# Scores of an attention head on its own 32 rows of the TensorE array, with three row maxima in the same tiling

## The chip, the cores and the metric

The kernel runs on one core of one Trainium2 chip. The metric is the time of one execution on the device in microseconds (us): 1010.03 us, the median of three runs (1009.28 to 1010.32). One execution was also recorded by the hardware profiler; everything said below of single instructions comes from that record.

## The reference

`x` is 2048 tokens by 448 features. Two attentions are computed from it, each with 16 heads of 28 features, and a gate per token mixes them:

```python
g = sigmoid((x * gate_w).sum(-1, keepdims=True))
a = A(x)     # linear attention: feature maps by two softmaxes per head, then (phi_k^T V), and a quotient
b = B(x)     # softmax attention, all 2048 queries against all 2048 keys, per head:
             #   scores = q @ k^T * 28 ** -0.5;  p = softmax(scores);  o = p @ v;  then @ wo
return g * a + (1 - g) * b
```

Only B is touched by the change. Everything is float32; a product in TensorE's fast format (fp32r) loses low bits, so each factor is split into a high and a low part, and a product of two such factors is high x high + low x high + high x low.

## The kernel before, in words

**Front** (up to about 356 us in the trace): projections of q, k and v, the whole of A, and the first part of the row maxima of B. **Attention loop** (the rest): B, head group by head group. A head group is four heads; a block (`gq`, 16 of them) is one head group with 512 queries; a step (`s`, 256 of them) is one block with 128 keys. Before the loop ends, the last head group's blocks are projected by `wo` (`project`, L1020) and mixed with A.

*Scores* (`scores`, L869). For each of the four heads j, one matmul over all 128 array rows makes scores transposed, 128 keys by 512 queries, in a PSUM bank `st`. The 128 rows are a stack (L840 to L864): 4 groups of 32 rows, which hold, beside the row of the maxima, the parts of k against the parts of q: high, low, high, low of k (`kst`) against high, high, low, low of q (`qst`). So one matmul of 128 rows yields all products of one head at once. Row 0 of `qst` holds the row maximum of each query and row 0 of `kst` holds -1, so that the maximum is subtracted in the same matmul. ScalarE then takes exp of each bank into an SBUF tile `p` (L890).

*Values* (`values`, L1008). For step s-1, four matmuls, each on its own 32 columns of the array (tile_position (0, 32j)), add p times v into one PSUM bank `pv` per block. The operands are plain float32, and the trace shows two passes per matmul, so eight records for one step.

*Row maxima*. The maximum over the 2048 keys must be known before a block's first score. It is taken from scores in one product (high x high, 28 rows). There are two kinds of work for it:
- A *unit* (`mx_unit`, L259) in the front: four matmuls on four groups of 32 array rows make two differences and two scores; ScalarE takes relu of the differences (L291) and VectorE adds and takes the maximum (L292). `NF` = 76 units are done before the loop.
- A *visit* (`mx_visit`, L307) in the loop: four matmuls (L324), one for each head, on four groups of 32 rows, for 128 queries by 512 keys. One bank in four goes by ScalarE (relu, L328) and is joined to another by VectorE (L333); the others are reduced by VectorE straight from PSUM (L336, L342). This uses keys that were differenced by GpSimd before (`take_diffs`). There are 180 visits.

When a block's maxima are complete, VectorE reduces and transposes them (`mx_reduce`, L238), and SyncE's DMA queue copies them into row 0 of `qst` in four DMAs (`load_nm`, L857).

*Order*. The order on TensorE, VectorE, ScalarE and GpSimd is the order of the program; SyncE's queue holds the DMAs. The main loop (L1146) goes by visits: steps 1 to 104 in pairs with one visit a pair, steps 105 to 232 alternately with 5 and 3 heads' scores ahead of a visit (`ahead`, L1145), the last ones in pairs with no visit. One round of it is: scores, values, visit. So TensorE goes through three tilings in a round: 128x128 (scores), 128 rows by 32 columns (values), 32 rows by 128 columns (visit). Of the 8 PSUM banks one is `pv`; the other seven go round among scores and visits (`cycle_banks`, L937).

At the end of a block (`finish`, L1052) VectorE copies `pv` out (L419), the denominators go through DRAM by three DMAs (L422, L433, L434) with a reciprocal on VectorE three steps later (L429), and GpSimd multiplies (L440).

Of the kernel before, what the change touches and what calls it, by code (L numbers as in the profile page):

```python
# [8 lines left out]
F32 = mybir.dt.float32  # L9
# [8 lines left out]
P = 128  # L18
# [11 lines left out]
NF = 76  # L30
LOWEST = -3.0e38
LAST = 232
OUTS = (200, 238, 246, 210)
PROJ = (235, 243, 251)
# [7 lines left out]
def gated_mix_kernel(ctx, tc, xT, wqkB, wvB, wvA, wkAT, wqAT, phi, woA, woB,  # L42
# [141 lines left out]
    diffs = []  # L184

    def mx_load(g, c):
        mxs[("kc", g, c)] = r = mx_tile("kc", f"kc{g}_{c}", 5)
        if c == 0:
            mxs["kd"] = mx_tile("kd", f"kd{g}", 1)
            for h in range(3):  # L190
                mx_rows(mxs["kd"], (h,), k_d[g], (h,), h * 512)
        for h in range(4):
            mx_rows(r, (h,), k_d[g], (h,), 512 * (c + (c == h and c < 3) - (c == h + 1 and c > 0)))
        if c < 3:
            js, t = slice(32 * c, 32 * c + DH), mxs["kd"]
            diffs.append((mxs["u"] + mxs["f"] // 4, lambda: nc.gpsimd.tensor_sub(
                r[js], f32(r[js]), f32(t[js]))))

    def take_diffs(n):
        while diffs and diffs[0][0] + n <= mxs["u"] + mxs["f"] // 4:  # L200
            diffs.pop(0)[1]()
# [33 lines left out]

    GM, QM = NF // 16, NF % 16 // 4

    def mx_reduce(gq):  # L238

        col = 64 * gq  # L240
        if gq < GM:
            parts = [(0, 4, col, 2)]
        elif gq == GM:
            parts = [(0, QM, col, 2), (QM, 4, col + 8 * QM, 4)]
        else:
            parts = [(0, 4, col, 4)]

        def reduce():
            for a, z, c, n in parts:
                nc.vector.tensor_reduce(  # L250
                    red[:, :16].rearrange("p (h t) -> p h t", t=4)[:, :, a:z],
                    part[:, c:c + 4 * (z - a) * n].rearrange("p (k t h) -> p h t k", t=z - a, h=4),
                    AX.X, ALU.max)
            nm_of[gq] = nm = mxp.tile([P, 32], F32, tag="nm", name=f"nm{gq}", bufs=7)
            nc.vector.transpose(nm, f32(red))

        mxs["fin"].append(reduce)

    def mx_unit():  # L259
# [5 lines left out]
        take_diffs(2)  # L265
# [3 lines left out]
        if gq < GM:  # L269
            c, qt = divmod(r, 4)  # L270
            hp, b = divmod(c, 2)
            col = 64 * gq + 16 * b + 4 * qt + 2 * hp
            if r in (4, 9):
                pair_query(gq + 1, r // 9)
        else:
            c, qt = divmod(r, QM)
            hp, b = divmod(c, 2)
            col = 64 * gq + 4 * QM * b + 4 * qt + 2 * hp
            if r == 0:
                mx_query(gq)  # L280
# [13 lines left out]
        if gq < GM and qt == 3 and qb == NQ - 1:  # L294
            pair_load(g + 1, c)
        if gq == GM and qt == QM - 1:
            mx_load(g, c)
        if r == 15:
# [3 lines left out]
    flats = [(GM, kb, qt, h, 64 * GM + 8 * QM + 4 * (4 - QM) * kb + 4 * (qt - QM) + h)  # L302
             for qt in range(QM, 4) for kb in range(4) for h in range(4)]
    flats += [(gq, kb, qt, h, 64 * gq + 16 * kb + 4 * qt + h) for gq in range(GM + 1, NG * NQ)
              for qt in range(4) for kb in range(4) for h in range(4)]

    def mx_visit(mid):  # L307


        take_diffs(2)  # L310
        f = mxs["f"]
        todo = flats[f:f + 4]
        fins = mxs["fin"][:1 if todo and todo[0][1] == 0 else None]
        del mxs["fin"][:len(fins)]
        mxs["f"] = f + len(todo)
        if todo:
            gq, kb, qt, _, col = todo[0]
            g, qb = divmod(gq, NQ)
            if kb == 1 and qt in (0, QM) and gq + 1 < NG * NQ and ("qc", gq + 1) not in mxs:
                mx_query(gq + 1)  # L320
            pm = mx_banks(f, kb)
            for j in sorted(range(4), key=lambda j: j != kb):
                js = slice(32 * j, 32 * j + DH)
                nc.tensor.matmul(pm[j], mxs[("qc", gq)][js, qt * P:(qt + 1) * P],  # L324
                                 mxs[("kc", g, kb)][js, :], start=True, stop=True,
                                 tile_position=(32 * j, 0))
            rl = late_p.tile([P, 512], F32, tag="rl", name=f"rl{f}", bufs=3)
            nc.scalar.activation(rl, pm[kb], AF.Relu if kb < 3 else AF.Copy)  # L328
            seen = 0
            for j in sorted({0, 1, 2, 3} - {kb}, key=lambda j: j == kb - 1):  # L330
                if j == kb - 1:
                    r = mxs["rl"]
                    nc.vector.tensor_tensor_reduce(r, pm[j], r, 1.0, LOWEST, ALU.add, ALU.max,  # L333
                                                   part[:, col + j:col + j + 1])
                else:
                    nc.vector.tensor_reduce(part[:, col + j:col + j + 1], pm[j], AX.X, ALU.max)  # L336
                seen += 1
                if seen == 2:
                    mid()
            mxs["rl"] = rl  # L340
            if kb == 3:
                mxs["fin"].append(lambda: nc.vector.tensor_reduce(  # L342
                    part[:, col + 3:col + 4], rl, AX.X, ALU.max))
            if qb == NQ - 1 and g + 1 < NG:
                if qt == 2 and kb == 3:
                    mx_load(g + 1, 0)
                if qt == 3 and kb < 3:
                    mx_load(g + 1, kb + 1)
            if qt == 3 and kb == 3:
                mx_reduce(gq)  # L350
        for fn in fins:
            fn()
# [487 lines left out]
    def stack(nm, keys):  # L840
        r = at.tile([P, 4, 512], F32R, name=nm)
        nc.gpsimd.memset(f32(r), 0.0)
        if keys:
            nc.gpsimd.memset(f32(r[0:1]), -1.0)
        return r

    def load_stack(r, src, c, parts):
        for b, i in enumerate(parts):
            nc.sync.dma_start(f32(r[32 * b + 4:32 * b + 32]),
                              src[:, i, c:c + 512].rearrange("(j d) n -> d j n", d=DH))  # L850
        return r

    def load_q(gq):
        g, qb = divmod(gq, NQ)
        qst_of[gq] = load_stack(qst[gq % 2], q_d[g], qb * 512, (0, 0, 1, 1))

    def load_nm(gq):  # L857
        nm = nm_of.pop(gq)
        row = f32(qst_of[gq][0:1].rearrange("p a (t b r) -> p (a t) b r", b=4, r=32))
        for b in range(4):  # L860
            nc.sync.dma_start(row[:, :, b, :], nm[32 * b:32 * b + 16, :])

    def load_k(g, kb):
        kst_of[(g, kb)] = load_stack(kst[(4 * g + kb) % 5], k_d[g], kb * 512, (0, 1, 0, 1))  # L864

    NS = NG * NQ * NT
    pv_of, pts, late, mids = {}, {}, {}, {}

    def scores(s, i, js=range(4)):  # L869

        gq, kt = divmod(s, NT)
        g, qb = divmod(gq, NQ)

        def score(j, st):
            nc.tensor.matmul(st, kst_of[(g, kt // 4)][:, j, (kt % 4) * P:(kt % 4 + 1) * P],  # L875
                             qst_of[gq][:, j, :], start=True, stop=True)

        if s == 0:
            for j in (2 * i, 2 * i + 1):
                p, st = at.tile([P, 512], F32, name=f"p{s}_{j}"), ps_mx(f"st{s}_{j}")  # L880
                score(j, st)
                nc.scalar.activation(p, st, AF.Exp, scale=SCALE)
                pts.setdefault(s, []).append(p)
            return
        sts = {j: bank(b, f"st{s}_{j}") for j, b in zip(js, i)}
        for j in js:
            score(j, sts[j])
        for j in js:
            p = late_p.tile([P, 512], F32, tag="p", name=f"p{s}_{j}", bufs=12)
            nc.scalar.activation(p, sts[j], AF.Exp, scale=SCALE)  # L890
            pts.setdefault(s, []).append(p)
# [10 lines left out]
    for t in range(8, NT):  # L902
# [5 lines left out]
        else:  # L908
            value_b(t, lambda i: scores(0, i // 3 - 1) if i in (4, 7) else None)
# [13 lines left out]
    late3, visit = [0, 1, 2], [3, 4, 5, 6]  # L923
    free = []
    spare = []
# [3 lines left out]


    for i in (0, None, 5, 4, 3, 2, 1, 6):
# [5 lines left out]
    def cycle_banks(n):  # L937

        x, y = late3[:], visit[:]
        if spare:  # L940
            b = [(free.append(free.pop(0)), free[-1])[1] for _ in range(n)]
        elif n == 4:
            b = x + y[:1]
            late3[:], visit[:] = [b[2], b[3], y[3]], [b[0], y[1], b[1], y[2]]
        elif n == 3:
            b = x
# [323 lines left out]
```

## Time and profile before

| what | before |
|---|---|
| time, median of 3 runs | 1010.03 us |
| span of the profiled execution, first to last instruction | 1008.5 us |
| time of TensorE matmuls in flight, share of the span | 1002.0 us, 99% |
| ScalarE | 821.3 us, 81% |
| VectorE | 647.5 us, 64% |
| GpSimd | 249.8 us, 25% |
| granted TensorE clock | 1.000 |

The profiled execution has no time of its own beside its span; 1010.03 is 1.5 us more than the span. PE stands for TensorE's matmuls and PEld for its weight loads, which can run beside them; DVE is VectorE, ACT ScalarE, POOL GpSimd, SP SyncE. A matmul's recorded duration reaches from its start to the modelled arrival of its last result, so matmuls overlap and a busy PE says little; start to start is what a matmul costs. Rows of the timeline merge instructions of one kind that follow each other: start, duration from the first start to the last end, engine, line, count, and in brackets the idle time before and what ended it.

### The profile page before, as it was taken

What the parts mean: (1) busy time and instruction counts of PE and PEld (TensorE: products, weight loads), DVE (VectorE), ACT (ScalarE), POOL (GpSimd) and SP (SyncE); (2) the same over time, 40 slices, a digit from 0 to 9 for tenths busy, and PEclk for the clock granted to TensorE, in tenths of its full rate; (3) what the DMA queues carried; (4) which work ended last, traced back from release to release, by engine and by line L of the source; (5) the groups of instructions that cost most, each with busy time, mean ns of one, the idle gap of its engine ahead of it and who ended that gap; (6) DMA issues with size and microseconds to landing.
All of it is one profiled execution on the core that took longest, in us unless ns stands there. A gap on an engine that the chain in (4) does not pass through costs nothing.

```text
span 1008.5 us, 18049 instructions
## 1 busy us (share of the span) xinstructions
PE 1002.0 (99%) x6344; PEld 565.2 (56%) x6344; DVE 647.5 (64%) x1336; ACT 821.3 (81%) x1614; POOL 249.8 (25%) x218
## 2 busy tenths in 40 slices
PE   9999999999999999999999999999999999999998
PEld 7777777877777754444444443333333333335665
DVE  5566777898764635445445468888888788885112
ACT  4455556587866699999999999999999999997662
POOL 1134545679635910310110110010120101100010
PEclk9999999999999999999999999999999999999999
DMA  9873010122233771223542334433232255610441
GB/s 303 300 249 108 32 52 32 43 56 81 80 103 95 174 146 37 67 63 80 113 101 49 72 76 94 107 71 71 68 79 63 68 124 141 148 38 30 137 147 56
DMA packets 64605, 99.64 MB, mean 99 GB/s; under 512 B 18166, under 2 KB 24934, under 8 KB 64514
## 3 DMA queue, kind: packets, MB, share of 16 engines
q1 hardware_dynamic: 64514, 98.49, 37.1%
q8 instruction: 50, 0.82, 0.3%
q14 instruction: 41, 0.34, 0.1%
HBM read 70.29 MB, written 27.78 MB: 97 GB/s over the span
## 4 chain that ended last, share of the span: by engine, by line
PE 92%; DVE 3%; DMA 3%; issue 1%; ACT 1%; SPq 0%; DVEq 0%; ACTq 0%
PE st L875 28%; PE pv L1015 24%; PE pm L324 8%; PE poa L109 4%; PE pk L127 4%; PE pva L127 4%; PE pqk L109 3%; PE pmd L287 3%; PE pob L109 3%; PE pq L109 2%; PE pvb L127 2%; PE pvb L109 2%; DMA qkd<-ev 2%; PE pn L553 1%; DMA xraw<-in_xT_dram 1%; PE pft L541 1%
## 5 line engine op out<-in xcount | busy, mean ns | idle before, releaser
L890 ACT ACTIVATE p<-st 128x512 f32<-128x512 f32 x1020 | 525.1, 639 | 26.4 <-PE st L875 26.4
L336 DVE TENSOR_REDUCE part<-pm 128x1 f32<-128x512 f32 x405 | 258.7, 685 | 179.3 <-PE pm L324 179.2
L875 PE MATMUL st<-qst,kst 128*128 128x512 f32 x1024 | 299.7, 423 | 0.0
L1015 PE MATMUL pv<-p,vb 128*32 128x512 f32 x2048 | 259.7, 601 | 0.0
L875 PEld LDWEIGHTS st<-qst,kst 128*128 128x128 f32 x1024 | 171.1, 187 | 101.3 <-ACT p L890 38.9
L440 POOL TENSOR_TENSOR oUb<-oUb,rsb 128x512 f32<-128x512 f32 x15 | 19.3, 1287 | 494.8 <-DMA rsb<-rdb 262.8
L292 DVE CUSTOM_DVE_ANT_0 rl<-pmb,rl 128x512 f32<-128x512 f32 x152 | 98.0, 682 | 46.6 <-ACT rl L291 46.5
L328 ACT ACTIVATE rl<-pm 128x512 f32<-128x512 f32 x180 | 111.5, 620 | 10.6 <-PE pm L324 10.2
L324 PEld LDWEIGHTS pm<-kc,qc 28*128 28x128 f32 x720 | 34.4, 181 | 150.9 <-ACT p L890 102.3
L291 ACT ACTIVATE rl<-pmd 128x512 f32<-128x512 f32 x152 | 82.9, 601 | 31.7 <-PE pmb L287 29.3
L1015 PEld LDWEIGHTS pv<-p,vb 128*32 128x32 f32 x2048 | 50.4, 108 | 96.2 <-issue 93.9
L333 DVE CUSTOM_DVE_ANT_0 rl<-pm,rl 128x512 f32<-128x512 f32 x135 | 91.8, 680 | 0.0
L324 PE MATMUL pm<-kc,qc 28*128 28x512 f32 x720 | 91.0, 495 | 0.0
L109 PE MATMUL pqk<-XH,wB 128*128 128x512 f32 x192 | 59.4, 397 | 0.8 <-DVE ev L593 0.8
L592 ACT CAST ev<-pqk 128x512 fp32r<-128x512 f32 x28 | 16.0, 588 | 38.9 <-PE pqk L109 21.9
L109 PE MATMUL poa<-woA_s,oTa 128*128 128x448 f32 x192 | 43.4, 375 | 0.0
L1026 DVE SCALAR_TENSOR_TENSOR acc<-pob,gate,acc 128x448 f32<-128x448 f32 x12 | 8.2, 684 | 50.8 <-PE pob L109 50.8
L109 PEld LDWEIGHTS pqk<-XH,wB 128*128 128x128 f32 x192 | 35.3, 188 | 9.8 <-issue 1.5
L287 PE MATMUL pmb<-kp,qp 28*128 28x512 f32 x152 | 39.8, 494 | 0.4
L127 PE MATMUL pk<-wkA_s,XH 128*128 128x448 f32 x128 | 39.4, 381 | 0.0
L109 PEld LDWEIGHTS poa<-woA_s,oTa 128*128 128x128 f32 x192 | 34.9, 188 | 6.2 <-issue 2.9
L593 DVE TENSOR_TENSOR ev<-pqk,ev 128x512 fp32r<-128x512 f32 x28 | 18.9, 689 | 29.9 <-ACT ev L592 29.8
(159 smaller groups left out, 1214.5 us busy)
## 6 DMA issues: line engine op xcount, KB each, us to landing
qkd<-ev SPq DMA_DIRECT2D x28, 512.0 KB
qst<-qkd SPq DMA_DIRECT2D x64, 224.0 KB
kst<-qkd SPq DMA_DIRECT2D x64, 224.0 KB
od<-oTb SPq DMA_DIRECT2D x48, 112.0 KB
rsa<-rda SPq DMA_DIRECT2D x8, 512.0 KB
rsb<-rdb SPq DMA_DIRECT2D x15, 256.0 KB
gad<-ga SPq DMA_DIRECT2D x16, 224.0 KB
acc<-gad SPq DMA_DIRECT2D x4, 896.0 KB
```

The costliest lines, as they stand in the source:

```text
L109: nc.tensor.matmul(dst, l, r, start=i == 0, stop=i == len(todo) - 1)
L127: nc.tensor.matmul(dst[:, :n], l, r, start=i == 0, stop=i == len(todo) - 1, skip_group_check=True)
L287: nc.tensor.matmul(pm[j], qc[js, qt * P:(qt + 1) * P], kc[js, :], start=True, stop=True, tile_position=(32 * i, 0))
L291: nc.scalar.activation(rl, pm[i], AF.Relu)
L292: nc.vector.tensor_tensor_reduce(rl, pm[2 + i], rl, 1.0, LOWEST, ALU.add, ALU.max, part[:, col + i:col + i + 1])
L324: nc.tensor.matmul(pm[j], mxs[("qc", gq)][js, qt * P:(qt + 1) * P], mxs[("kc", g, kb)][js, :], start=True, stop=True, tile_position=(32 * ...
L328: nc.scalar.activation(rl, pm[kb], AF.Relu if kb < 3 else AF.Copy)
L333: nc.vector.tensor_tensor_reduce(r, pm[j], r, 1.0, LOWEST, ALU.add, ALU.max, part[:, col + j:col + j + 1])
L336: nc.vector.tensor_reduce(part[:, col + j:col + j + 1], pm[j], AX.X, ALU.max)
L875: nc.tensor.matmul(st, kst_of[(g, kt // 4)][:, j, (kt % 4) * P:(kt % 4 + 1) * P], qst_of[gq][:, j, :], start=True, stop=True)
L890: nc.scalar.activation(p, sts[j], AF.Exp, scale=SCALE)
L1015: nc.tensor.matmul(pv[32 * j:32 * j + 32, :], vb[kt // 8][:, kt % 8, 4 * g + j, :], pt[j], start=kt == 0, stop=kt == NT - 1, tile_position ...
```

## The change

- The stacks now keep each head on its own 32 rows: row 32j the maxima, rows 32j+4 to 32j+31 the 28 features, with the high part in one plane and the low part in another. The tiles are half as large. `load_nm` fills a block's four rows by 16 DMAs of 4x32 instead of four of 16x32.
- The scores of a head are three matmuls of 32 rows that accumulate in one bank (`PASSES`: high x high, low k x high q, high k x low q), on the head's own row group; the passes of the four heads are interleaved, so that neighbours stand on different row groups.
- Row maxima in the loop: three a step (not four a visit), each one matmul of 28 rows on its head's row group, put among the scores' passes, and each reduced by VectorE straight from PSUM. ScalarE's relu of the loop, the joins on VectorE and the differences on GpSimd go.
- The loop goes one step at a time; `values` runs two steps behind (`LAG` = 2; one in the last steps) with 16 `p` tiles instead of 12. Seven PSUM banks go round by a fixed permutation.
- `NF` is 80: four more units in the front. The loop then has 704 maxima, three a step in steps 1 to 235. Projections begin at steps 237, 244 and 252.

The core of the diff (renamed helpers, the loop's bookkeeping and the old code's other lines are left out):

```diff
-NF = 76
+NF = 80
-LAST = 232
+LAG = 2
 OUTS = (200, 238, 246, 210)
-PROJ = (235, 243, 251)
+PROJ = (237, 244, 252)
...
+    def mx_score(item, pm):
+        gq, kb, qt, j, _ = item
+        js = slice(32 * j, 32 * j + DH)
+        nc.tensor.matmul(pm, mxs[("qc", gq)][js, qt * P:(qt + 1) * P],
+                         mxs[("kc", gq // NQ, kb)][js, :], start=True, stop=True,
+                         tile_position=(32 * j, 0))
+    def mx_done(item, pm):
+        gq, kb, qt, h, col = item
+        nc.vector.tensor_reduce(part[:, col:col + 1], pm, AX.X, ALU.max)
...
+    PASSES = ((0, 0), (1, 0), (0, 1))
+    def score(s, j, n, st):
+        gq, kt = divmod(s, NT)
+        k, q = PASSES[n]
+        js = slice(32 * j, 32 * j + 32)
+        nc.tensor.matmul(st[j], kst_of[(gq // NQ, kt // 4)][js, k, (kt % 4) * P:(kt % 4 + 1) * P],
+                         qst_of[gq][js, q, :], start=n == 0, stop=n == 2,
+                         tile_position=(32 * j, 0), skip_group_check=True)
...
+    def scores(s, todo):
+        if len(todo) == 3:
+            l0, l1, e0 = [x[3] for x in todo]
+            e1, = {0, 1, 2, 3} - {l0, l1, e0}
+            b = free[:]
+            free[:] = [b[2], b[0], b[3], b[1], b[6], b[4], b[5]]
+            b = [bank(i, f"g{s}_{n}") for n, i in enumerate(b)]
+            st, pm = {e0: b[0], e1: b[1], l0: b[4], l1: b[5]}, [b[2], b[3], b[6]]
+            for n in range(4):
+                for j in (e0, e1) if n < 3 else ():
+                    score(s, j, n, st)
+                for i, j in enumerate((l0, l1)):
+                    if n:
+                        score(s, j, n - 1, st)
+                    else:
+                        mx_score(todo[i], pm[i])
+            mx_score(todo[2], pm[2])
+            js = (e0, e1, l0, l1)
...
+        exps_of(s, js, st, late_p, tag="p", bufs=16)
+        for x, m in zip(todo, pm):
+            mx_done(x, m)
...
     def load_nm(gq):
         nm = nm_of.pop(gq)
-        row = f32(qst_of[gq][0:1].rearrange("p a (t b r) -> p (a t) b r", b=4, r=32))
-        for b in range(4):
-            nc.sync.dma_start(row[:, :, b, :], nm[32 * b:32 * b + 16, :])
+        for h in range(4):
+            row = f32(qst_of[gq][32 * h:32 * h + 1, 0, :].rearrange("p (t b r) -> p t b r", b=4, r=32))
+            for b in range(4):
+                nc.sync.dma_start(row[:, :, b, :], nm[32 * b + 4 * h:32 * b + 4 * h + 4, :])
...
+    for s in range(NS + 18):
...
+        if 0 < s < NS:
+            if s in mids:
+                mids.pop(s)()
+            scores(s, mx_next())
+        upto = s - LAG if s < NS - 2 else s - 1
+        while vals and vals[0] <= upto:
+            t = vals.pop(0)
+            values(t)
+            if t % NT == NT - 1:
+                finish(t // NT, s)
```

More of the change, by code (lines that the diff above doesn't have):

```diff
@@ L180, in mx_tile @@
         return mxp.tile([P, 512], F32R, tag=tag, name=nm, bufs=bufs)
-    diffs = []
     def mx_load(g, c):
[L187 to L201, printed above, removed]
+        mxs[("kc", g, c)] = mx_rows(mx_tile("kc", f"kc{g}_{c}", 5), range(4), k_d[g], range(4),
+                                    c * 512)
     def mx_query(gq):
@@ L315, in mx_visit @@
         mxs["f"] = f + len(todo)
[L316 to L350, printed above, removed]
@@ L863, in load_k @@
     def load_k(g, kb):
-        kst_of[(g, kb)] = load_stack(kst[(4 * g + kb) % 5], k_d[g], kb * 512, (0, 1, 0, 1))
+        kst_of[(g, kb)] = load_stack(kst[(4 * g + kb) % 5], k_d[g], kb * 512)
     NS = NG * NQ * NT
     pv_of, pts, late, mids = {}, {}, {}, {}
-    def scores(s, i, js=range(4)):
+    PASSES = ((0, 0), (1, 0), (0, 1))
+    def score(s, j, n, st):
         gq, kt = divmod(s, NT)
[L872 to L885, printed above, removed]
-        for j in js:
[L887 to L891, printed above, removed]
@@ new lines, in first_scores @@
+    def first_scores():
+        st = [ps_mx(f"st0_{j}") for j in range(4)]
+        for n in range(3):
+            for j in range(4):
+                score(0, j, n, st)
+        exps_of(0, range(4), st, at)
+    def scores(s, todo):
[16 more added lines that the diff above has]
+            js = (e0, e1, l0, l1)
+        else:
+            js = range(4)
+            n = 4 + len(todo)
+            b = free[:n]
+            free[:] = free[n:] + b[4:] + b[:4]
+            b = [bank(i, f"g{s}_{n}") for n, i in enumerate(b)]
+            st, pm = dict(enumerate(b[:4])), b[4:]
+            for n in range(3):
+                for j in js:
+                    score(s, j, n, st)
+            for x, m in zip(todo, pm):
+                mx_score(x, m)
+        exps_of(s, js, st, late_p, tag="p", bufs=16)
+        for x, m in zip(todo, pm):
+            mx_done(x, m)
@@ L918, in gated_mix_kernel, with take_bank @@
     ps2 = ctx.enter_context(tc.tile_pool(name="ps2", bufs=1, space=PSUM, reuse_waits="tile"))
[L923 to L925 removed]
+    free = [0, 1, 2, 3, 4, 5, 6]
     def bank(i, nm):
         return ps2.tile([P, 512], F32, tag=f"g{i}", name=nm, bufs=1)
[L931 removed]
+    def take_bank(nm):
+        free.append(free.pop(0))
+        return bank(free[-1], nm)
+    for i in (0, None, 1, 6, 5, 4, 3, 2):
         if i is None:
@@ L1038, in tail_open @@
     def tail_open():
-        tail["po"] = [bank(i, f"poL{n}")[:, :D]
-                      for n, i in enumerate([spare[0], free.pop(0), free.pop(0)])]
+        tail["po"] = [bank(free.pop(0), f"poL{n}")[:, :D] for n in range(3)]
         for tl in range(4):
```

182 lines of the change are left out of this document (61 added, 121 removed).

## The prediction

> **What bounds the kernel now.** I read the page's busy times first, then its chain of work, then busy times by stage, then the timeline of two rounds of the loop.
>
> ```profile
> span 1008.5 us, 18049 instructions
> PE 1002.0 (99%) x6344; PEld 565.2 (56%) x6344; DVE 647.5 (64%) x1336; ACT 821.3 (81%) x1614; POOL 249.8 (25%) x218
> ...
> PE 92%; DVE 3%; DMA 3%; issue 1%; ACT 1%; SPq 0%; DVEq 0%; ACTq 0%
> ```
>
> ```profile
> 354.00:589.00 235.00, 235.00 (x1472) 108.97 (x1470) 111.19 (x228) 234.85 (x476) 27.46 (x28) 1.00 0.37 82
> 589.00:918.00 329.00, 329.00 (x2041) 126.08 (x2040) 269.16 (x542) 318.64 (x638) 31.77 (x29) 1.00 0.37 86
> 918.00:992.00 74.00, 74.00 (x420) 45.73 (x412) 12.33 (x23) 47.54 (x94) 5.08 (x5) 1.00 0.34 110
> ```
>
> Columns of the stages: window, length, then PE, PEld, DVE, ACT, POOL busy, granted clock. TensorE is busy throughout and carries 92% of the chain, at clock 1.00. But ScalarE is at 235 of 235 us and 319 of 329 us of the two long stages: there are two bounds side by side, and an edit must relieve both. VectorE has room: 111 of 235, 269 of 329.
>
> Two rounds of the single-step stage (timeline; start, duration, engine, line, operation, count):
>
> ```profile
> 603.34 0.50 PE L324 MATMUL pm<-kc,qc 28*128 28x512 f32 x4
> 603.77 0.96 PE L875 MATMUL st<-qst,kst 128*128 128x512 f32 x3
> 603.90 0.66 ACT L328 ACTIVATE rl<-pm 128x512 f32<-128x512 f32 x1
> 603.92 1.29 DVE L336 TENSOR_REDUCE part<-pm 128x1 f32<-128x512 f32 x2 [0.38 <-PE pm L324]
> 604.38 1.65 ACT L890 ACTIVATE p<-st 128x512 f32<-128x512 f32 x3
> 604.67 1.06 PE L1015 MATMUL pv<-p,vb 128*32 128x512 f32 x8
> 605.67 0.50 PE L324 MATMUL pm<-kc,qc 28*128 28x512 f32 x4
> 606.10 1.48 PE L875 MATMUL st<-qst,kst 128*128 128x512 f32 x5
> 606.19 0.60 ACT L328 ACTIVATE rl<-pm 128x512 f32<-128x512 f32 x1 [0.16 <-PE pm L324]
> 606.69 2.55 ACT L890 ACTIVATE p<-st 128x512 f32<-128x512 f32 x5
> 606.84 0.32 PEld L875 LDWEIGHTS st<-qst,kst 128*128 128x128 f32 x2 [0.22 <-ACT rl L328]
> 607.50 1.07 PE L1015 MATMUL pv<-p,vb 128*32 128x512 f32 x8
> 608.50 0.51 PE L324 MATMUL pm<-kc,qc 28*128 28x512 f32 x4
> ```
>
> Two rounds take 608.50 - 603.34 = 5.16 us, 2.58 a step. On TensorE: pm start to st start 0.43, values to pm 1.00, scores the rest. ScalarE takes 10 instructions in 5.16 us; five exps take 2.55, so (2.55 - 0.64) / 4 = 0.48 each from start to start (0.64: mean of one, below).
>
> The loop from step 1 to the values of step 254:
>
> ```profile
> 356.35 2.27 PE L875 MATMUL st<-qst,kst 128*128 128x512 f32 x8
> ...
> 991.32 1.06 PE L1015 MATMUL pv<-p,vb 128*32 128x512 f32 x8
> ```
>
> That is 635.0 us; what lies ahead (356.4) and behind (17.2) is touched only in the front. The profiled execution's sum is made against 1008.5 us; the median is 1.5 us more, which I add.
>
> **The change part by part.** *TensorE, per step.* It removes 4 matmuls of 128 rows and two thirds to all of a visit; it adds 12 matmuls of 32 rows and 3 of 28. In the instruction order of the changed kernel a step is 15 matmuls in one tiling, then the values. Each row group gets 3 or 4 of the 15: four rounds. What is a round? Two matmuls of 512 columns that follow each other in full tiling:
>
> ```profile
> 76.01 0.39 PE L109 MATMUL pqk<-XL,wB 128*128 128x512 f32 x1
> ...
> 77.64 0.63 PE L109 MATMUL pqk<-XH,wB 128*128 128x512 f32 x2
> ```
>
> Between these two rows lie seven starts (one XL, two XH, and so on): 1.63 / 7 = 0.233 us. A visit's four matmuls on four row groups end together after 0.50 us, like one st after a change of tiling, so four row groups do run side by side. No row shows a second round behind the first. From below it is 0.233, from above the 0.43 of pm start to st start, which holds a change of tiling too. I take 0.233, the nearer case in kind (same columns, no change of tiling). Then TensorE needs 1.00 (values, with the changes) + 0.43 (one round, with the change out) + 3 x 0.233 = 2.13 us a step.
>
> In two sentences that the sum doesn't use: the Trainium skill, "TensorE: Matmul & The Clock Gate", Part 3, "Measured speedup vs the span model", gives 3.07 times for four row tiles of 512 columns, which as an estimate makes a round 4 x 0.233 / 3.07 = 0.30 and the time about 998 us (TensorE 1.43 + 3 x 0.30 = 2.34 a step). The visit's 0.50 shows no such loss in a single round, and no run here shows several.
>
> *ScalarE* loses one relu of five instructions and keeps 4 x 0.48 = 1.93 us a step. *VectorE* gets three reductions: two take 1.29, one 0.69, so 0.60 each, 1.8 a step. Both are under 2.13, and GpSimd loses work. *Banks.* Seven banks, seven results a step: each result waits for one of the step before.
>
> ```profile
> L890 ACT ACTIVATE p<-st 128x512 f32<-128x512 f32 x1020 | 525.1, 639 | 26.4 <-PE st L875 26.4
> ```
>
> In the diff's permutation the second late head's first pass takes the bank of the step before's third exp, and the last passes of the early heads stand behind it on TensorE. So there is a ring: three exps in a row (the row of three at 604.38: 1.65); the hand-over to TensorE (relu end 606.79 to weight load 606.84: 0.05); the waiting matmul and, right behind it, the early head's last pass on another row group, with weight load exposed (0.50); the hand-over to ScalarE (603.84 to 603.90: 0.06); then the next step's first exp. 1.65 + 0.05 + 0.50 + 0.06 = **2.26 us**, longer than TensorE's 2.13. I take 2.26 for steps 1 to 235: 531.1 us.
>
> *Ends of blocks.* VectorE's copy of `pv` comes once a block and has 2.26 - 1.8 = 0.46 of slack to hide in. With reciprocal and reduction I allow 0.3 us a block, 4.5 us in all (bounds 0, and 15 x 1.4 = 21 if the slack hides nothing):
>
> ```profile
> L419 DVE COPY oUb<-pv 128x512 f32<-128x512 f32 x8 | 5.5, 691 | 4.7 <-PE pv L1015 4.7
> L250 DVE TENSOR_REDUCE red<-part 128x16 fp32r<-128x64 f32 x8 | 2.0, 256 | 0.0
> L429 DVE RECIPROCAL denb<-denb 128x16 f32<-128x16 f32 x8 | 2.0, 248 | 0.0
> L255 DVE STREAM_TRANSPOSE nm<-red 128x32 f32<-128x32 f32 x8 | 1.7, 212 | 0.3
> ```
>
> *Steps 236 to 255* have no maxima. Before:
>
> ```profile
> 942.29 1.92 PE L1015 MATMUL pv<-p,vb 128*32 128x512 f32 x16
> ...
> 946.31 1.92 PE L1015 MATMUL pv<-p,vb 128*32 128x512 f32 x16
> ...
> 954.83 1.92 PE L1015 MATMUL pv<-p,vb 128*32 128x512 f32 x16
> ```
>
> A pair of steps takes 4.02 without and 8.52 with two projections: 2.01 and 4.26 a step. After, TensorE needs 1.00 + 0.43 + 2 x 0.233 = 1.90 and ScalarE 1.93. I take 1.95 for the 8 without and 4.26 - 0.11 = 4.15 for the 12 with: 65.4 us.
>
> *Front.* Four more units, each 0.63 us of TensorE:
>
> ```profile
> 70.61 0.37 PE L127 MATMUL pk<-wkA_s,XH 128*128 128x448 f32 x1
> 70.91 0.50 PE L287 MATMUL pmd<-kp,qp 28*128 28x512 f32 x2
> ...
> 71.34 0.47 PE L127 MATMUL pk<-wkA_s,XL 128*128 128x448 f32 x1
> 71.65 0.56 PE L127 MATMUL pk<-wkA_s,XH 128*128 128x448 f32 x2
> ...
> 338.06 0.50 PE L287 MATMUL pmd<-kp,qp 28*128 28x512 f32 x2
> ...
> 340.12 0.50 PE L287 MATMUL pmd<-kp,qp 28*128 28x512 f32 x2
> ```
>
> From 70.61 to 71.65 is 1.04 with a unit, and two matmuls of 448 columns take 0.41 without. They come into the last stretch, where units are now 2.06 apart. Bounds: 4 x 0.63 = 2.5 and 4 x 2.06 = 8.2. I take 3, since between units TensorE has other matmuls to run.
>
> *Maxima into the stack.*
>
> ```profile
> L861 SPq DMA_DIRECT2D qst<-nm x64: 502/587/836, 336.7 to 923.9; - x64
> ```
>
> Sixteen DMAs instead of four: 16 x 0.587 = 9.4 us of SyncE's queue a block. A block lasts 16 x 2.26 = 36 us, and in the queue's order they stand where the stack's tile comes free, most of a block ahead. The last block's maxima are done after step 235 and needed at 240: 1.95 + 3 x 4.15 = 14.4 us, enough. The denominators' DMA stands behind up to 13 of them, and its reader comes three steps (6.8 us) later. I cost it at nothing.
>
> *Sum.* 531.1 + 4.5 + 65.4 = 601.0 against 635.0: 34.0 less. The front gives back 3. 1008.5 - 31.0 = 977.5, and with 1.5: **979 us**.
>
> **The rivals.** *Weights of the same row group are not loaded ahead* (slower). Then each of the three later rounds shows its load, 0.50 - 0.39 = 0.11 (first matmul after a change against a following one): TensorE needs 2.13 + 0.33 = 2.46 a step, 0.20 over the forecast, 235 x 0.20 = 47: 1026 us. It decides from 0.087 a round, where a step costs (635.0 - 4.5 - 65.4 - 3) / 235 = 2.391 us. Against it: in column tiling, loads for busy column groups do run ahead, 16 rounds of four in 0.99 us with the loads in 0.85 us alongside:
>
> ```profile
> 126.21 0.99 PE L496 MATMUL pkv<-featk,vap 128*32 128x56 f32 x64
> ...
> 126.21 0.85 PEld L496 LDWEIGHTS pkv<-featk,vap 128*32 128x32 f32 x64 [0.25 <-issue]
> ```
>
> For it: no row shows it with row groups. The same page of the Trainium skill, Part 3, "The mechanism", says that LDWEIGHTS overlaps matmuls in flight only when the row group differs. By that rule this rival holds; the pkv rows, all on the same rows, speak against it as a general rule.
>
> *Four accumulating row groups are slower* (slower). A round between 0.32, from where it decides ((2.391 - 1.43) / 3), and 0.43: at 0.375 TensorE needs 2.555, 235 x 0.295 = 69: 1048 us. Only single rounds of non-accumulating matmuls speak against it.
>
> *The ring doesn't bind*, since TensorE takes pieces of it early: then 2.13, 235 x 0.13 = 31 less: 948 us. *The sixteen DMAs come late* (slower): 7 us more queue a block shown in full in 15 blocks, 105: 1084; it decides when the last row lands after the block's first score, and the order in the queue speaks against it.
>
> **How the numbers follow.** Forecast 0.60, ring doesn't bind 0.11, loads not ahead 0.14, slow rounds 0.08, late DMAs 0.04, and 0.03 for sums that meet near 1010. Faster 0.71, same 0.03, slower 0.26; 0.2%, 2 us, is about what a measurement here can tell from no change. The forecast's own range is 955 to 1000 (ends of blocks, front). To hold 8 in 10 it takes in 948 and 1026: 946 to 1028 leaves out the slow rounds and the late DMAs, 0.12, and a little of each edge.
>
> **What would show it.** Right: values 2.2 to 2.3 us apart through steps 1 to 235; PE starts on one row group 0.23 apart; PEld of the scores idle for ACT p once a step; ACT exps in fours with a gap of 0.3; no relu in the loop. Wrong: 0.34 between passes of a row group (loads), 0.3 or more with loads early (slow rounds), first scores of a block waiting on a DMA, or DVE with no idle time.

## The result and the profile after

| | before | after |
|---|---|---|
| time, median (17 runs each, taken alternately) | 1010.06 us (1009.09 to 1013.58) | 1006.43 us (1002.82 to 1011.8) |
| span of the profiled execution | 1008.5 us | 1002.8 us |
| granted clock of that execution | 1.000 | 0.994 |

The ratio is 0.9963, with a 95% interval of 0.9948 to 0.9978: 3.6 us faster, where 979 us were forecast. The direction was right; 27 of the 31 us that were to be won are missing. After's profiled execution is the fifth fastest of its 17 runs (1004.62 us); the sums below are made against its span.

From the page of the changed kernel, the rows that answer to those of before:

```profile
span 1002.8 us, 22531 instructions
PE 987.7 (98%) x8392; PEld 604.5 (60%) x8392; DVE 725.6 (72%) x1335; ACT 752.8 (75%) x1442; POOL 234.2 (23%) x224
...
PE 86%; DVE 6%; DMA 3%; SPq 2%; issue 1%; ACT 1%; POOL 1%; DVEq 0%; POOLq 0%; ACTq 0%
```

ScalarE gave up 68 us, as meant. But TensorE's part of the chain of waits fell from 92 to 86%, and SyncE's queue (SPq), which had nothing in it, now has 2%, VectorE 6%. Busy times by stage (after; steps 1 to 235 in two pieces, then 236 to 255; columns as before):

```profile
359.20:589.00 229.80, 224.50 (x2193) 114.48 (x2192) 184.70 (x305) 197.45 (x384) 23.06 (x24) 0.99 0.24 70
589.00:917.80 328.80, 324.76 (x3206) 165.20 (x3204) 270.97 (x449) 288.08 (x559) 26.70 (x25) 0.99 0.19 54
917.80:985.30 67.50, 67.50 (x536) 37.24 (x532) 9.94 (x17) 39.52 (x79) 5.08 (x5) 1.00 0.38 117
```

In steps 1 to 235 TensorE now stands still for 229.8 - 224.5 + 328.8 - 324.8 = 9.3 us, at a clock of 0.99, where it never did before. ScalarE is at 86 and 88% in the two pieces and VectorE at 80 and 82%, so neither is full, and a wait has to be looked for. The list of waits (after; us in total, times, longest) has a row that before's does not have:

```profile
DVE denb L383 <- DMA denb<-oUb: 20.8, 12, 6.0
```

VectorE's reciprocal of the denominators waits for their DMA in 12 of the blocks. The longest of these waits in the timeline, end of a block (after):

```profile
507.42 6.12 SPq L176 DMA_DIRECT2D kc<-qkd  x12
...
511.01 0.69 DVE L373 COPY oUb<-pv 128x512 f32<-128x512 f32 x1
...
513.64 3.50 SPq L804 DMA_DIRECT2D qst<-qkd  x4
...
517.18 4.75 SPq L817 DMA_DIRECT2D qst<-nm  x7
...
519.23 1.07 PE L976 MATMUL pv<-p,vb 128*32 128x512 f32 x8
522.04 0.60 SPq L376 DMA_DIRECT2D denb<-oUb  x1
522.68 5.54 SPq L817 DMA_DIRECT2D qst<-nm  x9
523.95 0.25 DVE L383 RECIPROCAL denb<-denb 128x16 f32<-128x16 f32 x1 [6.02 <-DMA denb<-oUb]
524.12 1.82 DVE L295 TENSOR_REDUCE part<-g 128x1 f32<-128x512 f32 x3
524.80 0.29 PEld L831 LDWEIGHTS g<-qst,kst 32*128 32x128 f32 x2 [5.41 <-DVE part L295]
524.80 0.79 PE L831 MATMUL g<-qst,kst 32*128 32x512 f32 x2 [4.50 <-DVE part L295]
...
527.57 1.94 PE L976 MATMUL pv<-p,vb 128*32 128x512 f32 x8
```

Read it from the copy of `pv`. It ends at 511.70, and the denominators could go out then. SyncE's queue goes on with what stands ahead: the last loads of keys for the row maxima (`kc`, until 513.54), the four loads of the query stack, then seven of the sixteen DMAs of the maxima, 0.68 us apart. The denominators' DMA is issued at 522.04, 10.3 us late. VectorE reached the reciprocal three steps after the copy, as the program says, and sat before it for 6.02 us; behind it in VectorE's order stand the three reductions of the maxima, which hold the PSUM banks that TensorE's next scores need. So TensorE stops for 4.50 us. Values start at 519.23 and again at 527.57: 8.34 us for a step of 2.3.

This block is the extreme. In the eleven others with a wait, the DMA goes out 4.9 to 7.1 us after the copy, and the reciprocal waits 0.55 to 2.98 us. In ten of them, 13 of the sixteen DMAs of the maxima go first, as here (after; 11 in the row shown, and two before it):

```profile
742.95 0.69 DVE L373 COPY oUb<-pv 128x512 f32<-128x512 f32 x1
743.75 6.84 SPq L817 DMA_DIRECT2D qst<-nm  x11
750.69 0.58 SPq L376 DMA_DIRECT2D denb<-oUb  x1
752.85 0.25 DVE L383 RECIPROCAL denb<-denb 128x16 f32<-128x16 f32 x1 [2.98 <-DMA denb<-oUb]
753.70 0.50 PE L831 MATMUL g<-qst,kst 32*128 32x512 f32 x2 [1.66 <-DVE part L295]
```

The stall has a second part. After the long stop the first score takes 0.79 us instead of 0.50 and the values 1.94 instead of 1.07: the granted clock is 0.50 from 524.1 to 530.9. By windows (after), the piece with this stall between two without, and the piece with the stop at 752:

```profile
480.00:520.00 40.00, 39.93 (x399) 20.17 (x391) 31.98 (x54) 35.38 (x69) 3.17 (x3) 1.00 0.28 83
520.00:560.00 40.00, 35.50 (x330) 17.19 (x326) 28.90 (x47) 29.24 (x58) 3.18 (x3) 0.91 0.20 54
560.00:600.00 40.00, 40.00 (x406) 20.87 (x404) 33.29 (x56) 35.80 (x70) 3.17 (x3) 1.00 0.19 51
720.00:760.00 40.00, 38.16 (x368) 19.00 (x364) 30.78 (x50) 32.58 (x64) 3.40 (x4) 0.96 0.26 73
```

The granted clock is 0.91 there and 1.00 around it. In the last piece it is 0.96: 0.50 from 756.2 to 759.6, after a stop of only 1.66 us. The Trainium skill, "TensorE: Matmul & The Clock Gate", Part 1, "What's actually happening", says that TensorE falls to half its clock after an idle window of about 3.4 us; the stop of 4.5 us with 1.94 against 1.07 us behind it agrees, and the stop of 1.66 us, shorter than that and followed by half the clock all the same, does not.

In all, the steps from values to values that took over 2.6 us add up to 17.4 us more than the usual ones (steps 1 to 232). The usual ones take 2.30 us. After's runs spread over 9 us, e1's below over 2. The granted clock recorded with each run of after goes along: 0.993 to 0.997 in the four shortest, 0.987 to 0.989 in the three longest. So the stops probably differ from one execution to the next; only one of these executions has a trace.

### The profile page after: what moved, and what is told of

Same layout as the page of the kernel before. It is cut to its first block, busy times and chain, and to the rows that moved or that the text cites. A ratio compares the mean times of both kernels' runs of the same rounds, so it can differ in the third digit from the quotient of the medians.

```text
span 1002.8 us, 22531 instructions
## 1 busy us (share of the span) xinstructions
PE 987.7 (98%) x8392; PEld 604.5 (60%) x8392; DVE 725.6 (72%) x1335; ACT 752.8 (75%) x1442; POOL 234.2 (23%) x224
## 4 chain that ended last, share of the span: by engine, by line
PE 86%; DVE 6%; DMA 3%; SPq 2%; issue 1%; ACT 1%; POOL 1%; DVEq 0%; POOLq 0%; ACTq 0%
PE g L831 27%; PE pv L976 24%; PE pqk L109 4%; PE pk L127 4%; PE poa L109 4%; PE pva L127 4%; PE g L288 3%; PE pob L109 3%; PE pmd L260 3%; PE pvb L127 2%; DVE part L295 2%; SPq L817 2%; DMA denb<-oUb 2%; PE pvb L109 1%; PE pq L109 1%
## 5 line engine op out<-in xcount | busy, mean ns | idle before, releaser
L839 ACT ACTIVATE p<-g 128x512 f32<-128x512 f32 x1020 | 526.1, 607 | 101.2 <-PE g L831 101.0
L295 DVE TENSOR_REDUCE part<-g 128x1 f32<-128x512 f32 x704 | 441.6, 682 | 82.9 <-PE g L288 80.5
L831 PEld LDWEIGHTS g<-qst,kst 32*128 32x128 f32 x3060 | 221.2, 184 | 226.9 <-DVE part L295 207.4
L831 PE MATMUL g<-qst,kst 32*128 32x512 f32 x3060 | 345.5, 423 | 8.9 <-DVE part L295 8.1
L976 PE MATMUL pv<-p,vb 128*32 128x512 f32 x2048 | 274.5, 608 | 0.0
L288 PE MATMUL g<-kc,qc 28*128 28x512 f32 x704 | 233.3, 496 | 0.5
L288 PEld LDWEIGHTS g<-kc,qc 28*128 28x128 f32 x704 | 87.0, 183 | 3.0 <-DVE part L295 2.6
L976 PEld LDWEIGHTS pv<-p,vb 128*32 128x32 f32 x2048 | 40.6, 108 | 68.5 <-issue 67.3
L260 PE MATMUL pmd<-kp,qp 28*128 28x512 f32 x160 | 40.0, 495 | 0.0
L127 PE MATMUL pva<-wvA_s,XH 128*128 128x450 f32 x128 | 37.8, 371 | 0.0
```

Source lines behind the costliest of these rows:

```text
L127: nc.tensor.matmul(dst[:, :n], l, r, start=i == 0, stop=i == len(todo) - 1, skip_group_check=True)
L260: nc.tensor.matmul(pm[j], qc[js, qt * P:(qt + 1) * P], kc[js, :], start=True, stop=True, tile_position=(32 * i, 0))
L288: nc.tensor.matmul(pm, mxs[("qc", gq)][js, qt * P:(qt + 1) * P], mxs[("kc", gq // NQ, kb)][js, :], start=True, stop=True, tile_position=(3 ...
L295: nc.vector.tensor_reduce(part[:, col:col + 1], pm, AX.X, ALU.max)
L831: nc.tensor.matmul(st[j], kst_of[(gq // NQ, kt // 4)][js, k, (kt % 4) * P:(kt % 4 + 1) * P], qst_of[gq][js, q, :], start=n == 0, stop=n == ...
L839: nc.scalar.activation(p, st[j], AF.Exp, scale=SCALE)
```

## The experiments

The theory after the result: the sixteen DMAs are late for a reader that the forecast had thought safe (VectorE's reciprocal), and without them the loop would run regularly at 2.30 us a step. Rivals: the sixteen DMAs are harmless and something in the tiling makes TensorE stop; or the gain of the tiling is small and came from ScalarE. What was run, times beside the kernel before on the same chips; "step" is the mean from values to values over steps 1 to 232, without gaps above 2.6:

| run | median, us | ratio to before, 95% interval | step, us |
|---|---|---|---|
| the change | 1006.43 | 0.9948 to 0.9978 | 2.30 |
| e1_nm4: four DMAs of the maxima a block | 986.69 | 0.9749 to 0.9782 | 2.30 |
| e7_8_dmas: eight | 985.76 | 0.9745 to 0.9774 | 2.30 |
| e2_reader_late: sixteen, the reader three steps later | 987.93 | 0.9763 to 0.9803 | 2.30 |
| e6_before_16_dmas: the kernel before with sixteen | 1020.02 | 1.0086 to 1.0120 | |
| e8_values_one_behind: four, `LAG` = 1 | 987.79 | 0.9764 to 0.9793 | 2.30 |
| e4_plain_order: four, passes in plain order | 1004.93 | 0.9936 to 0.9965 | 2.38 |
| e5_stacked_scores: four, scores by 128 rows | 1048.65 | 1.0366 to 1.0397 | 2.56 |
| e3_extra_on_act: four, a copy after the second exp | 996.06 | 0.9849 to 0.9878 | 2.34 |
| e9_extra_before_fourth: four, the copy after the third | 996.22 | 0.9825 to 0.9874 | 2.34 |
| e10_half_exps: four, exps of half the columns | 971.05 | 0.9581 to 0.9629 | 2.23 |

### The DMAs

**e1_nm4.** The four rows of the stack lie 32 partitions apart, so one DMA can fill all four:

```diff
-        for h in range(4):
-            row = f32(qst_of[gq][32 * h:32 * h + 1, 0, :].rearrange(...))
-            for b in range(4):
-                nc.sync.dma_start(row[:, :, b, :], nm[32 * b + 4 * h:32 * b + 4 * h + 4, :])
+        row = f32(qst_of[gq][0:P:32, 0, :].rearrange("p (t b r) -> p t b r", b=4, r=32))
+        for b in range(4):
+            nc.sync.dma_start(row[:, :, b, :], nm[32 * b:32 * b + 16, :])
```

> The changed kernel with the four rows of maxima copied by four DMAs instead of sixteen, nothing else. Queue theory: in the changed kernel the copy of the denominators stands behind the small DMAs on SyncE's queue, is issued 6 to 10 us after VectorE's copy of pv instead of at once, and VectorE's reciprocal waits for it (20.8 us in 12 waits) with the reductions behind it. Steps 1 to 235 took 556.5 us where 235 regular steps of 2.30 are 540. With four DMAs the waits go: about 990 to 994 us, the granted clock back at 1.000 and the spread of the times under 2 us. Rival: the waits come from the landing time of the DMAs or from the order on VectorE, not from the number: 1003 to 1009 us, waits as before.

Measured: 986.69 us, 19.7 less than the change as it was, and 3 less than the least that was expected. Page, then SyncE's queue over the same block as above:

```profile
span 985.4 us, 22287 instructions
...
PE 95%; DVE 3%; issue 1%; ACT 0%; SPq 0%; DMA 0%; POOL 0%; DVEq 0%; POOLq 0%; ACTq 0%
```

```profile
505.52 3.85 SPq L804 DMA_DIRECT2D qst<-qkd  x4
509.42 2.34 SPq L816 DMA_DIRECT2D qst<-nm  x4
511.87 0.83 SPq L176 DMA_DIRECT2D qc<-qkd  x2
512.79 0.58 SPq L376 DMA_DIRECT2D denb<-oUb  x1
```

The queue has passed the maxima by 511.76, and the denominators go out at 512.79. The wait of VectorE for `denb` is gone from the list of waits, TensorE carries 95% of the chain, and none of steps 1 to 232 takes over 2.6 us. The spans of the two profiled executions differ by 17.4 us (1002.8 and 985.4), which is what after's long steps added up to. The four DMAs move the same bytes; 12 fewer instructions a block are worth 2% of the kernel.

**e2_reader_late** leaves all sixteen and moves what waits for them:

```diff
-        late.setdefault(s + 3, []).append(f2)
-        late.setdefault(s + 7, []).append(f3)
-        late.setdefault(s + 8, []).append(lambda: acts.append(f4))
+        d = 3 if gq < 14 else 0
+        late.setdefault(s + 3 + d, []).append(f2)
+        late.setdefault(s + 7 + d, []).append(f3)
+        late.setdefault(s + 8 + d, []).append(lambda: acts.append(f4))
```

> The changed kernel with its sixteen DMAs, but the reciprocal, the product and the split of a block's end three steps later (not for the last block, whose projection waits for them). Queue theory, that the only harm of the late copy is VectorE's wait: the longest wait was 6.0 us and three steps are 6.9 us, so it goes and the time is that of four DMAs within 2 us, 990 to 994 us. Rival, that the sixteen DMAs also make something else late (rows of maxima, keys): the time stays 5 us or more above that of four DMAs.

Measured: 987.93 us, nearly the whole of e1's gain with every DMA still there. In the list of waits one of twelve is left:

```profile
DVE denb L383 <- DMA denb<-oUb: 0.8, 1, 0.8
```

So the loss was the reader's wait, not the traffic and not the tiling.

**e7_8_dmas** (two rows a DMA: `32 * h:32 * h + 33:32` for h in 0, 2, and `nm[32 * b + 4 * h:32 * b + 4 * h + 8, :]`).

> The changed kernel with eight DMAs of 8x32 for the rows of maxima. Theory: the denominators' copy is issued 8 x 0.59 = 4.7 us earlier than with sixteen, so 1.5 to 5.5 us late instead of 6 to 10; with about 2 us of landing its reader, some 7 us after VectorE's copy, waits in few blocks or none: 986 to 990 us. Rival, that any number above four is felt: 995 or more.

Measured: 985.76 us, no different from four. The cost isn't proportional to the number: below some count the queue is through in time, and above it the step stops. It is, with e1, the best version that the runs found without leaving work out.

**e6_before_16_dmas** gives the kernel before the same number:

```diff
-        for b in range(4):
-            nc.sync.dma_start(row[:, :, b, :], nm[32 * b:32 * b + 16, :])
+        for h in range(4):
+            for b in range(4):
+                nc.sync.dma_start(row[:, 4 * h:4 * h + 4, b, :], nm[32 * b + 4 * h:32 * b + 4 * h + 4, :])
```

> The kernel before with its rows of maxima copied by sixteen DMAs of 4x32 instead of four of 16x32. Theory, it is the place in the queue that hurts: there the maxima's DMAs wait for the maxima themselves, late in a block, and the denominators' copy does not stand behind them, so nothing waits: within 3 us of the kernel before. Rival, sixteen small DMAs a block cost by themselves: 10 us or more slower.

Measured: 1020.02 us, 10 us more than before: the expectation missed, and the time came out at its rival's edge. But the wait is another one than in the changed kernel. In the chain of waits of this kernel (start, duration, what) the 16 issues follow each other, 0.62 us apart, and end so:

```profile
857.97 0.57 SPq L862
858.55 0.04 issue
858.59 1.57 DMA qst<-nm
860.16 0.14 issue
860.29 0.70 PE st L876 x2
```

Here the first scores of the block wait for the last row of the maxima. The profiled execution is 5.5 us longer than before's. It has such gaps of 0.2 to 1.2 us at five starts of blocks, 1.4 us in the front, and 1.0 us at step 106, where TensorE waited for a difference of keys on GpSimd (`kc`, L196), which stood behind a product that had waited for the denominators; whether the sixteen DMAs bring that one about was not tested. The three other runs took 1019 to 1022 us at granted clocks of 0.996 to 0.998, where the profiled one had 1.000, so they probably had longer stops; no trace shows these. Sixteen DMAs on this queue hurt both kernels; who pays depends on what stands behind them or waits for them.

### The tiling

**e5_stacked_scores** takes back the tiling of the scores alone (stacks of 128 rows and one matmul a head, as before; three maxima a step, four DMAs; 11 `p` tiles, since the stacks are larger):

```diff
-            for n in range(4):
-                for j in (e0, e1) if n < 3 else ():
-                    score(s, j, n, st)
...
+            for j in (e0, e1, l0, l1):
+                nc.tensor.matmul(st[j], kst_of[...][:, j, ...], qst_of[gq][:, j, :], start=True, stop=True)
+            for x, m in zip(todo, pm):
+                mx_score(x, m)
```

> One part undone: scores again as one matmul of 128 rows for each head on the old stacks (with four DMAs for the maxima, as they were there), all else as changed: three maxima a step in row groups after the scores, no relu, values two steps behind, 80 units. Banks go round so that first heads find banks freed early; 11 p tiles, since the old stacks need the room. Theory, the rounds of row groups are where the gain comes from: TensorE needs 1.00 (values, changes) + 0.34 + 2 x 0.233 + 0.32 (scores, change) + 0.43 (maxima, change) = 2.55 a step, 0.25 over the 2.30 of four DMAs alone, so about 59 us over it: 1040 to 1055 us. Rival, the gain comes from ScalarE's fifth instruction going: within 10 us of four DMAs alone.

Measured: 1048.65 us, 62 us over e1. Two steps in the timeline:

```profile
584.82 1.20 PE L828 MATMUL g<-qst,kst 128*128 128x512 f32 x4
...
585.94 0.50 PE L288 MATMUL g<-kc,qc 28*128 28x512 f32 x3
...
586.38 1.06 PE L968 MATMUL pv<-p,vb 128*32 128x512 f32 x8
...
587.37 1.20 PE L828 MATMUL g<-qst,kst 128*128 128x512 f32 x4
```

Relu, joins and differences are gone here too, and the kernel is slower than before. So relieving ScalarE alone doesn't give the gain; it needs the scores' rounds on row groups. Whether these would give it with ScalarE as full as before, no run tests. The four scores are 1.12 us from their start to that of the maxima, the maxima 0.44 more, the values 0.99: TensorE goes through three tilings in every step, where before it did so once in two steps up to step 104.

**e4_plain_order** keeps the tiling and runs the passes of all four heads in plain rounds, the maxima last, with the permutation of the banks that fits:

```diff
-            for n in range(4):
-                for j in (e0, e1) if n < 3 else ():
+            for n in range(3):
+                for j in (e0, e1, l0, l1):
                     score(s, j, n, st)
-                for i, j in enumerate((l0, l1)):
...
+            for x, m in zip(todo, pm):
+                mx_score(x, m)
```

> With four DMAs, the same 15 matmuls a step in plain order: first passes of four heads, second, third, then the three maxima; banks go round so that first passes find banks freed early. Same work on every engine. Ring theory: all four heads end one round later and the third exp's bank is asked for at once, so a step costs 2.39 instead of 2.30: 20 to 28 us over four DMAs alone. Rival, the order of the passes doesn't matter since TensorE has the same work: within 3 us of it.

Measured: 1004.93 us, 18 over e1 (20 to 28 expected), and a step of 2.38 against the 2.39 expected. The staggered order, which releases two heads to ScalarE a round earlier, is worth 0.08 us a step, together with the places of the maxima and the permutation of the banks that go with it.

**e8_values_one_behind** (`LAG` = 1).

> With four DMAs, and values one step behind the scores as before the change, instead of two. Ring theory: the values of step s-1 then wait for that step's fourth exp, but the last maximum of step s, which stands ahead of them on TensorE, waits for the same exp already: within 3 us of four DMAs alone. Rival, two steps are needed to keep ScalarE out of TensorE's path: 10 us or more over it.

Measured: 987.79 us, 1.1 more than e1. The second step of lag is worth next to nothing.

### What sets a step of 2.30

**e3_extra_on_act** tests the ring that the prediction named, by lengthening its row of three exps:

```diff
             nc.scalar.activation(p, st[j], AF.Exp, scale=SCALE)
+            if s and j == list(js)[1]:
+                nc.scalar.copy(junk, ident[:, :64])
```

> With four DMAs, and one small copy (128x64, SBUF to SBUF) on ScalarE between the second and the third exp of each step; it makes nothing that is used. Estimated at 0.15 to 0.2 us each. Ring theory (three exps, hand-over, waiting pass, hand-over set the step of 2.30): the ring grows by 0.08 to 0.13 a step, the time by 20 to 30 us over four DMAs alone, although ScalarE has 2.30 - 1.93 = 0.37 us of room a step. Rival, TensorE's own time sets the step: under 3 us more.

Measured: 996.06 us, 9.4 over e1: between the two expectations, so neither holds as it was put. The copy takes ScalarE 0.134 us and the step grows by 0.04. **e9_extra_before_fourth** puts the same copy where the three exps of that ring do not see it (`list(js)[2]`).

> The changed kernel with four DMAs of the maxima a block, and the same small copy of 128x64 on ScalarE as in e3_extra_on_act, here between the third and the fourth exp of each step (its result is not used). If the step is set by a ring over two steps that goes through all four exps (4.57 us per two steps, so 2.29 a step), the copy's 0.134 us comes once in two steps: 4.70 / 2 = 2.35 a step, +12 to +16 us over the 986.7 of e1_nm4, 997 to 1003. If it is set by the ring of the prediction, through three exps, or by TensorE alone, the copy lies in ScalarE's slack: the step stays at 2.30 and the time within 3 us of e1_nm4.

Measured: 996.22 us, the same as e3, and just under the 997 of the longer ring. Its timeline:

```profile
584.62 1.07 PE L978 MATMUL pv<-p,vb 128*32 128x512 f32 x8
585.57 0.26 ACT L840 COPY junk<-ident 128x64 f32<-128x64 f32 x1
...
586.80 1.06 PE L978 MATMUL pv<-p,vb 128*32 128x512 f32 x8
588.05 0.26 ACT L840 COPY junk<-ident 128x64 f32<-128x64 f32 x1
...
589.29 1.07 PE L978 MATMUL pv<-p,vb 128*32 128x512 f32 x8
```

Steps alternate, 2.18 and 2.49. If the prediction's ring of three exps had set the 2.30, e3's copy inside it would have made 2.43; the step was 2.34. And the copy costs the same on either side of the third exp, outside that ring too. So a longer ring through ScalarE binds in e3 and e9. One that comes round in two steps, which share one copy, would fit: two steps of e1 take 4.60 us, two of e9 4.68, which is 0.08 of the 0.134 more, as if such a ring had 0.05 us to spare in e1. This is argued from the numbers; no run isolates that ring. It would be 4.54 us or 2.27 a step, so what makes the 2.30 of e1 stays open.

**e10_half_exps** relieves ScalarE instead:

```diff
-            nc.scalar.activation(p, st[j], AF.Exp, scale=SCALE)
+            nc.scalar.activation(p[:, :256], st[j][:, :256], AF.Exp, scale=SCALE)
...
-                             pt[j],
+                             pt[j][:, :256].unsqueeze(1).to_broadcast([P, 2, 256]),
```

> The changed kernel with four DMAs of the maxima a block; from step 1 on each exp takes only the first 256 of a bank's 512 columns, and the values read these 256 twice, so that TensorE has the same number of columns to take and VectorE the same work, while ScalarE has about half (half of the attention's weights are left out of the result). If rings through ScalarE set the step and TensorE by itself needs the prediction's 2.13 us, the step falls from 2.30 to 2.13 to 2.2: 235 x 0.10 to 0.17 = 24 to 40 us less than the 986.7 of e1_nm4, 947 to 963. If TensorE's own work is what takes 2.30, the step stays and the time is within 5 us of e1_nm4; in between, the step is what TensorE needs by itself.

Measured: 971.05 us, 15.6 under e1, step 2.23: part of the way to 2.13, and outside the 947 to 963 that were expected. TensorE by itself, in a step of this run where it did not wait:

```profile
585.94 0.50 PE L830 MATMUL g<-qst,kst 32*128 32x512 f32 x2
...
586.05 0.43 PEld L830 LDWEIGHTS g<-qst,kst 32*128 32x128 f32 x8
586.28 0.64 PE L830 MATMUL g<-qst,kst 32*128 32x512 f32 x8
...
586.74 0.39 PE L288 MATMUL g<-kc,qc 28*128 28x512 f32 x1
...
587.09 1.07 PE L975 MATMUL pv<-p,vb 128*32 128x512 f32 x8
588.08 0.50 PE L830 MATMUL g<-qst,kst 32*128 32x512 f32 x2
```

The four rounds start at 585.94, 586.28, (one between, merged) and 586.74: the second and third take 0.46 together, 0.23 each. From the first round of one step to that of the next is 2.14 us, the prediction's 2.13; of e10's steps a quarter take 2.12 to 2.15. The load of the second round begins at 586.05, while the first round on the same row groups is in flight until 586.44. So rings through ScalarE cost 0.07 us a step in e1; another 0.10 above TensorE's own 2.13 is left with ScalarE half idle, and I did not take it apart.

## Why the prediction was wrong in size and right in kind

- **The step that failed** is "The denominators' DMA stands behind up to 13 of them, and its reader comes three steps (6.8 us) later. I cost it at nothing." It is worth 20 us (1006.43 - 986.69). The count was right (13 go first in ten of the twelve blocks), and so was the reader; the queue's time and the reader's were not set against each other. The reader comes 6.2 us after the copy's end. The DMA goes out 4.9 to 7.1 us after it, 10.3 in the block where loads of keys and of the stack stood ahead as well, and lands about 2 us later, so it is late in all twelve. The rival with the late DMAs looked only at the scores' first use of the rows, which is what happens in e6, and not here. Its price also left out the halved clock that follows a stop.
- **TensorE's 2.13 us a step** was right for a step in which it does not wait (2.14 in e10, whose mean is 2.23), and with it the round of 0.233. The rivals "loads not ahead" and "slow rounds" fall on the same rows. The Trainium skill, "TensorE: Matmul & The Clock Gate", Part 3, "The mechanism", says in its list of what overlaps that a load overlaps only matmuls on other row groups, though its paragraph above the list also names a background weight buffer. The load at 586.05 above, under matmuls of its own row groups, shows that the list does not hold here. The round that was estimated at 0.30 us from the 3.07 times of the Trainium skill, same page, Part 3, "Measured speedup vs the span model", took 0.23.
- **The ring of 2.26** was nearly the right size (2.30) for a wrong reason, which is luck. That rings through ScalarE bear on the step holds: e3, e9 and e10 each move it. That the one through three exps sets it falls with e3 (2.34 where it would have made 2.43) and e9. The difference of 0.04 is 9 us over 235 steps.
- **Ends of blocks** at 4.5 us: e1's mean step of 2.30 has them in, and none of its steps at a block's end is over 2.6, so no row gives them a cost of their own. Its steps 1 to 235 take 540.1 us against the 535.6 forecast for ring and ends together.
- **Steps 236 to 255**: 67.5 us against 65.4. A step with a projection takes 4.33 us, not 4.15, and one without 1.90, not 1.95. I took the saving of such a step from the old one with all else kept. But the projection multiplies by 128 rows, as the scores did before:

```profile
920.15 1.91 PE L109 MATMUL pob<-woB_s,oL 128*128 128x448 f32 x8
...
922.60 0.97 PE L831 MATMUL g<-qst,kst 32*128 32x512 f32 x12
```

  From the projection to the scores is 2.45 us, where before a projection added 4.26 - 2.01 = 2.25. A change of tiling that the old order did not have would explain it; no run isolates it.
- **The front** was right: the first scores of step 1 come 2.9 us later, 3 forecast.
- **The relief of both engines** was right as far as it goes: ScalarE, 235 of 235 us in the first stage before, is at 197 of 230. But e5 shows that relieving it does not give the gain by itself. Nor was there a gain in that stage: before, a pair of its steps took 4.45 us with four maxima, 2.22 a step, and after a step takes 2.30 with three. The gain is in steps 105 to 232, where two steps took 5.16 us and now take 4.60.

With the queue set right (e1) the forecast of 979 us would have missed by 8.

## What to carry to other kernels

When a change raises the number of DMAs on a queue, add up the issue times of everything that can stand ahead of each other DMA there, and compare the sum with the distance in time to that DMA's reader, for every reader, not only for that of the DMAs added. Splitting a transfer by rows need not multiply its DMAs: a strided partition range kept it at four, and that was 20 us. When several engines are near their bound, look for rings over two steps as well as one; a small copy put at two places in an engine's order tells which of its instructions the ring contains.

## What the runs showed of the hardware that was not expected

- A stop of TensorE of 4.5 us costs more than itself: the eight matmuls of the values after it took 1.94 us instead of 1.07, and the granted clock of a 40 us window fell to 0.91. After a stop of 1.66 us, with small gaps behind it, the clock was halved for 3.4 us too.
- Three accumulating matmuls on each of four row groups of 32 run at 0.23 us a round for all four (e10), the same as one full matmul of 512 columns (0.233 before), with their loads hidden.
- DMAs of the maxima take SyncE's queue 0.58 to 0.68 us each on the mean of a series, whether they carry 2 KB or 0.5: 2.34 us for four of 16x32 in e1, 9.98 us for sixteen of 4x32 in e6, 4.75 us for seven of 4x32 after.
